# A gated linear scan with top-1 expert routing on one core: second expert product turned round, late zero fills in narrow pieces, expert 0's first product ahead of the branch

## The chip, the cores and the metric

The kernel runs on one core of a Trainium2 chip. Five engines work from queues of their own and wait for each other by semaphores: PE (TensorE, matrix products), DVE (VectorE), ACT (ScalarE), POOL (GpSimd) and SP (SyncE, which here only issues DMAs). The metric is the device time of one execution in microseconds, the median of several runs; smaller is better. One execution was also recorded by the hardware profiler, and all rows below come from it.

## What is computed

The first half is an elementwise recurrence over time, `h = a_t * h + x_gated` per batch row and channel, on arrays of 4 x 5056 x 256 float32. Its result, seen as 20224 tokens of 256 numbers, goes to a layer of 8 experts that keeps at most 80 tokens per expert, those with the largest gate weight; all other rows of the output are zero:

```python
a_t = np.exp(log_a)                       # log_a = 8 * sigmoid(r) * log(sigmoid(a_param))
x_gated = np.sqrt(np.maximum(1.0 - a_t * a_t, 1e-6)) * sig_i * x
for t in range(S):
    h = a_t[:, t] * h + x_gated[:, t]
    y[:, t] = h
...
expert_idx = np.argmax(x @ w_gate, axis=1)          # x: the y of above, one row per token
for e in range(E):
    tok_idx = np.where(expert_idx == e)[0]          # cut to the 80 with the largest gate weight
    h = np.maximum(x[tok_idx] @ w1[e], 0.0)         # 256 -> 1024
    out[tok_idx] = gate_w[tok_idx, None] * (h @ w2[e])   # 1024 -> 256
```

## The kernel before

The time axis is cut into units, 20 of 1024 steps and at the two ends halves and a quarter (u20 has 512 steps, u21, the last, 256). For each unit the kernel loads r, i and x with tokens along the partitions, and does, in this order of dependence: A (PE turns r to channels along the partitions, in two halves, line 123), after tanh T on ACT (line 117); E (ACT takes the exponential into the state array Y, line 126); Q (POOL squares, line 129); S (ACT's square root, line 133); I (ACT's tanh of the i gate, line 137); U (POOL multiplies by x, line 140); B (PE turns the gated input, lines 147 and 148); N (DVE multiplies by the norm, line 151); Y (DVE's scan, line 161). The results stay on the chip in `Y`, 25 slots of [128, 2, 1024]. Steps l and c compute gate weights and expert choices, D stands for PE transposes that keep PE busy and are thrown away (line 231). What comes after what on each engine is the list `ORDER`, written out by hand; a letter with a unit and a half (`E20.0`) is one step.

**Zero fills.** The 20.7 MB of output are first filled with zeros by DMAs from SP's queue, in places that `ORDER` names with Z. A wide fill (line 209) writes 512 tokens, 512 KB, and reads 1024 zeros per partition from `Y[:, 19, 0]`, the slot in which the state of u20 and u21 will stand. A narrow fill (line 215) writes 256 tokens, 256 KB, from the last 256 columns of the same row (`h0`, columns 768 and up), which no unit overwrites. The step `E20.0` sets `st['last']` when its turn in the list comes, so that fills that stand behind it are narrow. `E20.0` and its scan write columns 0 to 511 of that row, and so have to wait until the wide fills have read it. SP's DMAs use eight semaphores in turn, so that a DMA waits for the eighth one before it, and at most eight are under way.

**Choice.** The 16 largest weights of each group are found early and late and combined; the result is `chosen` (token and weight for each slot of each expert).

**Experts.** `front` turns `chosen` into token columns (`col`) and weights (`AT`), with 30 thrown-away transposes on PE behind (`WARM[3]`, line 352). Then the token vectors are gathered: for an expert, ACT copies 32 columns, POOL 24, DVE 24 (`copies`, lines 511 and 512) with addresses that `fetch` (line 505) has loaded into registers. `front` does that for experts 0 and 1. A branch (line 605) then takes the usual case. In `experts`, expert k's `first` is 32 calls of [128 x 64] weights (w1) by 80 tokens, the two 64-column halves of the array side by side (line 550), with `relu` in halves on ACT and DVE (lines 566, 565). `second` is 32 calls in the same shape with w2 as the weights (line 560); its result has channels along the partitions, so ACT copies it to SBUF (`take`, line 567), PE turns it (`turn`, line 571), DVE multiplies by the gate weight (`weigh`, line 573) and POOL scatters 80 rows to the output (line 576). Weights are 2 MB per expert in two buffers; w1 of expert k+2 is asked for when `first(k)` is done, w2 by halves when `second(k)` is. An fp32 product call shows as two MATMULs in the trace (64 for 32 calls), a transpose as one.

Of the kernel before, what the change touches and what calls it, by code (L numbers as in the profile page):

```python
# [64 lines left out]
def moe_kernel(ctx, tc, x, r_gate, i_gate, a_param, w_gate, w1, w2, out, capacity=80):  # L65
# [471 lines left out]
    def experts(own):  # L537

        ps_f = own.enter_context(tc.tile_pool(name="ps_f", bufs=1, space=bass.MemoryType.PSUM))
        hbuf = [rows[:, :FC * CAP], rows[:, FC * CAP:2 * FC * CAP]]  # L540
        turned = [scr[:, (8 + 2 * k) * CAP:(10 + 2 * k) * CAP].rearrange("p (h s) -> p h s", h=2) for k in range(2)]
        res = [scr[:, 1024:1280], scr[:, 1280:1536], scr[:, 1536:1792], scr[:, 1792:2048]]
        phs, pos, outs, sent = {}, {}, {}, []
        def hidden(e): return hbuf[e % 2].rearrange("p (c s) -> p c s", c=FC)
        def first(e, half):
            ph = phs[e, half] = ps_f.tile([P, FC // 2, CAP], F32, name="ph", bufs=3)
            for c in range(half * FC // 2, (half + 1) * FC // 2):
                for h in range(2):
                    for j in range(0, P, P // 2):
                        nc.tensor.matmul(ph[j:j + P // 2, c % (FC // 2)], w1v(e)[:, h, c * P + j:c * P + j + P // 2], XG[:, e % 4, h],  # L550
                                         start=(h == 0), stop=(h == 1), tile_position=(0, j))
            if half and e + 2 < E:
                for g in range(2): load_w1(e + 2, g)
# [26 lines left out]
        for k in range(E):  # L580
            g = k + 2
            if k: take(k - 1)
            if 0 < k < E - 1: copies('A', g - 1, 16, 24)
            first(k, 0); relu(k, 0)
            if 0 < k < E - 1: copies('A', g - 1, 24); copies('V', g - 1, 20)
            first(k, 1); relu(k, 1)
            if k: turn(k - 1); weigh(k - 1)
# [49 lines left out]
```

## Time and profile before

| | us |
|---|---|
| median of 3 runs | 305.67 (305.45 to 306.17) |
| profiled execution | 306.08 |
| its span, first to last instruction | 304.3 |
| PE / DVE / ACT / POOL busy | 252.0 / 210.5 / 230.1 / 202.4 |
| DMA queue of SP | 99.63 MB, 87.1% of 16 engines' span |

All engines are busy about 70 to 80% of the span, so the shares alone name no bound. The kernel has three stretches. From 0 to about 220 us the units run, with the DMA engines busy nearly all the time. From about 220 to 248 us the last choice is made in short dependent steps, with no DMA from 234 us on. From 248 us to the end the eight experts run. A timeline row has the start, the duration (of a group: from its first to its last end), the engine, the line, the operation and its operands, the number, and in brackets the idle time ahead of it and what ended that.

### The profile page before, as it was taken

The page shows a single profiled execution, that of the slowest core. Times are in us where ns is not written, and L with a number is a line of the kernel's source. Part 1 is how long each engine was busy: PE and PEld are TensorE (multiplying, and loading weights), DVE is VectorE, ACT ScalarE, POOL GpSimd, SP SyncE. Part 2 cuts the span into 40 slices and gives each one's busy share as a digit, 9 for nine tenths or more (in the row PEclk, how much of TensorE's full clock was granted, in tenths as well). Part 3 has the DMA queues.
Part 4 walks back from the last instruction along what each step waited for, and adds up shares of the span by engine and source line. Part 5 has one row for each costly group of instructions (what it writes and reads, how often), then busy time and mean ns, then how long its engine had stood idle before and what let it go on. Part 6 is the DMA issues. An engine that isn't in the chain of part 4 may idle for free.

```text
span 304.3 us, 9900 instructions
## 1 busy us (share of the span) xinstructions
PE 252.0 (83%) x3748; PEld 228.0 (75%) x3748; DVE 210.5 (69%) x435; ACT 230.1 (76%) x443; POOL 202.4 (67%) x289
## 2 busy tenths in 40 slices
PE   4968899999899998999799798508979586996882
PEld 3767788898899897988788787407868486986871
DVE  2022069989999999999779889960779566566520
ACT  6999999999989999998998994607703366666510
POOL 2349999899999799899767488032305366777212
PEclk9999999999999999999999999955999787999997
DMA  6999999999999999889999999999997004999941
GB/s 235 407 412 408 409 411 407 408 408 408 407 416 412 365 364 323 325 313 381 409 357 401 310 369 416 408 363 329 308 346 259 1 4 167 300 382 384 360 150 32
DMA packets 38438, 100.99 MB, mean 332 GB/s; under 512 B 3056, under 2 KB 17264, under 8 KB 38384
## 3 DMA queue, kind: packets, MB, share of 16 engines
q1 hardware_dynamic: 38000, 99.63, 87.1%
q8 instruction: 31, 0.51, 0.7%
q0 software_dynamic: 384, 0.66, 0.7%
q14 instruction: 23, 0.19, 0.2%
HBM read 78.91 MB, written 21.36 MB: 330 GB/s over the span
## 4 chain that ended last, share of the span: by engine, by line
ACT 23%; DVE 18%; issue 14%; POOL 13%; DMA 12%; PE 11%; SPq 5%; POOLq 3%; DVEq 0%; ACTq 0%
DVE Y L161 8%; ACT Y L126 8%; POOL Y L512 6%; DVE pu L151 6%; ACT Y L117 5%; SPq L215 4%; ACT Y L133 4%; DMA out_dram<-Y 4%; DMA Y<-in_x_dram 4%; PE pr L123 3%; ACT Y L137 3%; POOLq L505 3%; DMA Y<-in_i_gate_dram 3%; POOL Y L129 2%; PE pu L147 2%
## 5 line engine op out<-in xcount | busy, mean ns | idle before, releaser
L140 POOL TENSOR_TENSOR Y<-Y 128x2048 f32<-128x2048 f32 (+2 forms) x22 | 90.9, 4142 | 20.7 <-DMA Y<-in_x_dram 14.4
L161 DVE TENSOR_TENSOR_SCAN Y<-Y,pu 128x1024 f32<-128x1024 f32 (+8 forms) x50 | 93.3, 1882 | 1.4 <-DMA out_dram<-Y 0.5
L129 POOL TENSOR_TENSOR Y<-Y 128x2048 f32<-128x2048 f32 (+2 forms) x22 | 71.6, 3260 | 28.7 <-ACT Y L126 18.7
L151 DVE SCALAR_TENSOR_TENSOR pu<-Y,pu 128x1024 f32<-128x1024 f32 (+2 forms) x44 | 48.6, 1111 | 52.8 <-PE pu L148 44.7
L148 PE MATMUL pu<-ident,Y 128*128 128x128 f32 x316 | 71.7, 274 | 3.4 <-POOL Y L140 3.4
L147 PE MATMUL pu<-ident,Y 128*128 128x128 f32 x316 | 72.6, 275 | 1.3 <-DVE Y L161 0.5
L123 PE MATMUL pr<-ident,Y 128*128 128x128 f32 x316 | 46.1, 289 | 24.3 <-ACT Y L126 20.0
L123 PEld LDWEIGHTS pr<-ident,Y 128*128 128x128 f32 x316 | 35.8, 146 | 32.6 <-ACT Y L126 27.7
L126 ACT ACTIVATE Y<-pr,tiny 128x1024 f32<-128x1024 f32 (+2 forms) x44 | 49.0, 1113 | 5.6 <-PE pr L123 5.3
L147 PEld LDWEIGHTS pu<-ident,Y 128*128 128x128 f32 x316 | 44.6, 141 | 4.8 <-issue 2.3
L148 PEld LDWEIGHTS pu<-ident,Y 128*128 128x128 f32 x316 | 44.6, 141 | 4.6 <-POOL Y L140 4.6
L231 PE MATMUL pl<-ident 128*128 128x128 f32 x287 | 42.6, 295 | 2.4 <-POOL ident masks.py:199 1.6
L137 ACT ACTIVATE Y<-Y 128x2048 f32<-128x2048 f32 (+2 forms) x22 | 38.2, 1736 | 4.7 <-DMA Y<-in_i_gate_dram 4.6
L511 ACT COPY Y<-Y 128x2 f32 x256 | 26.5, 191 | 18.5 <-issue 10.2
L117 ACT ACTIVATE Y<-Y 128x2048 f32<-128x2048 f32 (+2 forms) x22 | 38.1, 1736 | 2.7 <-DMA Y<-in_r_gate_dram 2.7
L241 PE MATMUL pl<-Y 128*32 128x64 f32 (+2 forms) x1344 | 39.0, 280 | 1.1 <-DVE lg L245 1.1
L231 PEld LDWEIGHTS pl<-ident 128*128 128x128 f32 x287 | 36.5, 154 | 3.2 <-POOL ident masks.py:199 1.6
L133 ACT ACTIVATE Y<-Y 128x2048 f32<-128x2048 f32 (+2 forms) x22 | 37.4, 1734 | 0.7 <-POOL Y L129 0.6
L241 PEld LDWEIGHTS pl<-Y 128*32 128x32 f32 x1344 | 33.9, 124 | 4.6 <-issue 3.2
L512 POOL COPY Y<-Y 128x2 f32 x192 | 24.4, 198 | 11.5 <-issue 6.9
L512 DVE COPY Y<-Y 128x2 f32 x192 | 22.6, 176 | 12.0 <-issue 12.0
L550 PE MATMUL ph<-Y 128*64 128x80 f32 x512 | 20.5, 233 | 4.9 <-issue 4.8
(126 smaller groups left out, 221.9 us busy)
## 6 DMA issues: line engine op xcount, KB each, us to landing
Y<-in_r_gate_dram SPq DMA_DIRECT2D x18, 1024.0 KB, 12.1
Y<-in_x_dram SPq DMA_DIRECT2D x18, 1024.0 KB, 9.3
Y<-in_i_gate_dram SPq DMA_DIRECT2D x18, 1024.0 KB, 9.7
Y<-in_moe_w_dram SPq DMA_DIRECT2D x32, 512.0 KB, 7.2
out_dram<-Y SPq DMA_DIRECT2D x28, 512.0 KB, 9.9
out_dram<-Y SPq DMA_DIRECT2D x23, 256.0 KB, 4.5
Y<-in_r_gate_dram SPq DMA_DIRECT2D x3, 512.0 KB
Y<-in_i_gate_dram SPq DMA_DIRECT2D x3, 512.0 KB
```

The costliest lines, as they stand in the source:

```text
L117: nc.scalar.activation(r, r, AF.Tanh, scale=0.5)
L123: nc.tensor.transpose(pr[:, c0:min(n, g + 512):nb], rr[:, at:at + P], ident)
L126: nc.scalar.activation(state(u, h), prs.pop((u, h))[:, :UNITS[u][2]], AF.Exp, scale=L[:, h:h + 1], bias=L[:, h:h + 1])
L129: nc.gpsimd.tensor_tensor(halves('r', u), a, a, op=ALU.mult)
L140: nc.gpsimd.tensor_tensor(i, i, flat('x', u), op=ALU.mult)
L147: nc.tensor.matmul(cols, xx[:, at:at + P], ident, start=True, stop=False, is_transpose=True)
L148: nc.tensor.matmul(cols, ii[:, at:at + P], ident, start=False, stop=True, is_transpose=True)
L151: nc.vector.scalar_tensor_tensor(pu, halves('r', u)[:, h], 0.5e-3, pu, op0=ALU.max, op1=ALU.mult)
L161: nc.vector.tensor_tensor_scan(y[:, s0:s1], y[:, s0:s1], q[:, s0:s1], init, op0=ALU.mult, op1=ALU.add)
L231: for _ in range(n): nc.tensor.transpose(spare, ident, ident)
L241: nc.tensor.matmul(pl[32 * j:32 * j + 32, s % 2, c0:c0 + n // NR], gates(h, b), Y[:, p, h, o + 4 * j + b:o + n:NR], start=(b == 0 and h == ...
L512: else: eng.tensor_copy(dst, src)
```

## The change

Four things are done.

1. In `ORDER` the fills from `A19.1` on are written z, which is `zero_fill(2)`: two narrow fills in place of one wide. `st['last']` goes. On SP's queue, from the last wide fills that stay to the first expert weights, before:

```order
L209 DMA out_dram<-Y 128x1024 x6
L109 DMA Y<-in_i_gate_dram 128x1024
L109 DMA Y<-in_r_gate_dram 128x1024
L113 DMA Y<-in_r_gate_dram 128x512
L209 DMA out_dram<-Y 128x1024 x4
L109 DMA Y<-in_x_dram 128x1024
L209 DMA out_dram<-Y 128x1024 x5
L113 DMA Y<-in_i_gate_dram 128x512
L113 DMA Y<-in_x_dram 128x512
L215 DMA out_dram<-Y 256x1x256 x22
L304 DMA Y<-in_moe_w_dram 128x1024 x2
```

and after:

```order
L208 DMA out_dram<-Y 128x1024 x6
L109 DMA Y<-in_i_gate_dram 128x1024
L109 DMA Y<-in_r_gate_dram 128x1024
L113 DMA Y<-in_r_gate_dram 128x512
L214 DMA out_dram<-Y 256x1x256 x8
L109 DMA Y<-in_x_dram 128x1024
L214 DMA out_dram<-Y 256x1x256 x10
L113 DMA Y<-in_i_gate_dram 128x512
L113 DMA Y<-in_x_dram 128x512
L214 DMA out_dram<-Y 256x1x256 x22
L303 DMA Y<-in_moe_w_dram 128x1024 x2
```

The nine wide fills around u20's x load became 18 narrow ones in the same places. On ACT, at the table load ahead of `E20.0` (the brackets name the semaphores waited for; DMAHW are the eight of SP's DMAs), before:

```order
L133 ACTIVATE Y<-Y 128x2048 [waits Pool_49]
L126 ACT_TABLE_LOAD [waits DMAHW4_49,DMAHW3_49,DMAHW5_49,DMAHW2_49,DMAHW6_49,DMAHW1_49,DMAHW7_49,DMAHW0_49]
L126 ACTIVATE Y<-pr,tiny 128x512 [waits PE_49] x2
L126 ACTIVATE Y<-pr,tiny 128x256 [waits PE_49]
L133 ACT_TABLE_LOAD
```

and after:

```order
L132 ACTIVATE Y<-Y 128x2048 [waits Pool_49]
L125 ACT_TABLE_LOAD [waits DMAHW5_49,DMAHW6_49,DMAHW4_49,DMAHW7_49,DMAHW0_49]
L125 ACTIVATE Y<-pr,tiny 128x512 [waits PE_49] x2
L125 ACTIVATE Y<-pr,tiny 128x256 [waits PE_49]
L132 ACT_TABLE_LOAD
```

`E20.0` (the 128x512 row) waited there for eight DMA semaphores, and now for five; the narrow fills don't read what it writes.

2. `second` holds relu's result as the weights, [128 x 80], and moves w2, 256 columns: 8 calls per expert in place of 32. Its result has tokens along the partitions; `take` and `turn` go, and `weigh` reads the product from PSUM.

3. `first(0)` stands in `front`, ahead of the branch, and `relu(0)` ahead of the copies for expert 1 (its result goes to a buffer of its own, `hbuf[2]`); the small steps on slots (`rows_of_slots`) move ahead of both. On PE, from the thrown-away transposes to expert 1, before:

```order
L352 MATMUL pd<-ident 128x128 x30
L533 TENSOR_LOAD lg
L605 COMPARE_AND_BRANCH
L550 MATMUL ph<-Y 64x80 x32
L560 MATMUL po<-rows,Y 64x80 x32
L550 MATMUL ph<-Y 64x80 x32
L571 MATMUL pd<-ident,Y 80x128 x2
L560 MATMUL po<-rows,Y 64x80 x32
```

and after (L351 the transposes, L527 first, L562 second):

```order
L351 MATMUL pd<-ident 128x128 x26
L527 MATMUL ph<-Y 64x80 x32
L549 TENSOR_LOAD lg
L598 COMPARE_AND_BRANCH
L562 MATMUL po<-Y 80x256 x8
L527 MATMUL ph<-Y 64x80 x32
L562 MATMUL po<-Y,rows 80x256 x8
```

The branch moved from ahead of expert 0's first product to behind it, and the transposes between the products are gone.

4. `WARM[3]` is 26 in place of 30. In the loop `weigh(k-1)` stands ahead of `first(k)`, and the loads of w1 behind `relu(k, 1)`.

The diff, without what repeats:

```diff
-WARM = (4, 45, 6, 30)
+WARM = (4, 45, 6, 26)
...
-E21.1 I21 N20.0 Z Q21 D5 B20.1 S21.1 c4.1 Y20.0 l19 U21 Z N20.1 c4.2 B21.0 Z Y20.1 c4.3 Z D5 B21.1 N21.0 l20 c4.4 N21.1 Y21.0 Z Y21.1 c4.5
+E21.1 I21 N20.0 z Q21 D5 B20.1 S21.1 c4.1 Y20.0 l19 U21 z N20.1 c4.2 B21.0 z Y20.1 c4.3 z D5 B21.1 N21.0 l20 c4.4 N21.1 Y21.0 z Y21.1 c4.5
...
-        if UNITS[u][0] == PAIRS - 1: st['last'] = True
...
-            if wide and N - a >= 512 and not st.get('last'):
+            if wide and N - a >= 512:
...
+             'l': logits, 'D': idle, 'Z': lambda: zero_fill(1, True), 'z': lambda: zero_fill(2), 'w': gate_weights}
...
+    hbuf = [rows[:, :FC * CAP], rows[:, FC * CAP:2 * FC * CAP], scr[:, 1024:1024 + FC * CAP]]
+    phs = {}
+    def hidden(e): return hbuf[e % 2 if e else 2].rearrange("p (c s) -> p c s", c=FC)
...
-        for k in 'APV': fetch(k, 1); copies(k, 1)
         rows_of_slots()
+        for half in range(2): first(0, half, ps, 2)
+        for k in 'APV': fetch(k, 1)
+        for half in range(2): relu(0, half)
+        for k in 'APV': copies(k, 1)
...
-            if half == 0: pos[e] = ps_f.tile([P, 2, 512], F32, name="po", bufs=2)
+            if half == 0: pos[e] = ps_f.tile([CAP, D], F32, name="po", bufs=2)
             for c in range(half * FC // 2, (half + 1) * FC // 2):
-                for h in range(2):
-                    for j in range(0, P, P // 2):
-                        nc.tensor.matmul(pos[e][j:j + P // 2, h, :CAP], w2v(e)[:, c, h * P + j:h * P + j + P // 2], hidden(e)[:, c],
-                                         start=(c == 0), stop=(c == FC - 1), tile_position=(0, j))
+                nc.tensor.matmul(pos[e], hidden(e)[:, c], w2v(e)[:, c], start=(c == 0), stop=(c == FC - 1))
...
-        def take(e): nc.scalar.copy(turned[e % 2], pos.pop(e)[:, :, :CAP])
-        def turn(e):
-
-            outs[e] = ps_f.tile([CAP, 2 * P], F32, name="pd")
-            for h in range(2): nc.tensor.transpose(outs[e][:, h * P:h * P + P], turned[e % 2][:, h], ident)
         def weigh(e):
-            nc.vector.tensor_scalar_mul(res[e % 4][:CAP], outs.pop(e), AT[:, E + e:E + e + 1])
+            nc.vector.tensor_scalar_mul(res[e % 4][:CAP], pos.pop(e), AT[:, E + e:E + e + 1])
...
+            if k:
+                if k < E - 1: copies('A', g - 1, 16, 24)
+                weigh(k - 1)
+                first(k, 0, ps_f, 3); relu(k, 0)
+                if k < E - 1: copies('A', g - 1, 24); copies('V', g - 1, 20)
+                first(k, 1, ps_f, 3); relu(k, 1)
             if g < E:
+                for h in range(2): load_w1(g, h)
                 for q in 'APV': fetch(q, g)
                 copies('A', g, 0, 16); copies('V', g, 0, 20); copies('P', g)
             if k: scatter(k - 1)
             second(k, 0); second(k, 1)
-        take(E - 1); turn(E - 1); weigh(E - 1); scatter(E - 1)
+        weigh(E - 1); scatter(E - 1)
```

## Rows read from the trace of the kernel before

**Rows 1.** busy time by stretch: us, engines' busy time, granted clock, DMA share, GB/s

```profile
198.00:200.00 2.00, 0.00 (x0) 0.00 (x0) 2.00 (x2) 0.00 (x0) 2.00 (x1) 0.67 1.01 414
...
210.00:212.00 2.00, 2.00 (x11) 2.00 (x11) 0.00 (x0) 1.97 (x3) 0.83 (x1) 0.50 1.05 350
...
234.00:236.00 2.00, 2.00 (x19) 1.81 (x17) 1.97 (x9) 1.43 (x8) 1.46 (x7) 1.00 0.02 8
...
250.00:255.00 5.00, 1.69 (x31) 1.53 (x29) 3.15 (x25) 3.22 (x30) 3.27 (x28) 0.83 0.58 213
...
270.00:275.00 5.00, 4.05 (x99) 3.45 (x94) 3.40 (x24) 3.20 (x31) 3.73 (x25) 1.00 1.06 390
```

**Rows 2.** timeline, ACT: start, duration, line, operation, idle before and releaser

```profile
193.78 1.91 ACT L133 ACTIVATE Y<-Y 128x2048 f32<-128x2048 f32 x1
...
204.75 1.28 ACT L126 ACT_TABLE_LOAD   x1 [9.06 <-DMA out_dram<-Y]
...
211.47 1.06 ACT L133 ACTIVATE Y<-Y 128x1024 f32<-128x1024 f32 x1
...
215.08 0.62 ACT L137 ACTIVATE Y<-Y 128x512 f32<-128x512 f32 x1
```

**Rows 3.** timeline, POOL, same stretch

```profile
197.94 2.34 POOL L140 TENSOR_TENSOR Y<-Y 128x1024 f32<-128x1024 f32 x1 [7.89 <-DMA Y<-in_x_dram]
...
208.94 1.89 POOL L129 TENSOR_TENSOR Y<-Y 128x1024 f32<-128x1024 f32 x1 [8.66 <-issue]
...
216.62 1.30 POOL L140 TENSOR_TENSOR Y<-Y 128x512 f32<-128x512 f32 x1
```

**Rows 4.** timeline, PE, same stretch (MATMULs alone)

```profile
193.00 1.15 PE L231 MATMUL pl<-ident 128*128 128x128 f32 x9
...
209.34 4.14 PE L231 MATMUL pl<-ident 128*128 128x128 f32 x23
```

**Rows 5.** timeline, DVE, same stretch

```profile
214.46 0.69 DVE L151 SCALAR_TENSOR_TENSOR pu<-Y,pu 128x512 f32<-128x512 f32 x1 [11.89 <-PE pu L148]
...
219.53 0.81 DVE L151 SCALAR_TENSOR_TENSOR pu<-Y,pu 128x256 f32<-128x256 f32 x2
```

**Rows 6.** timeline of SP's DMA queue, same stretch

```profile
190.17 4.61 SPq L209 DMA_DIRECT2D out_dram<-Y  x5
...
197.74 21.71 SPq L215 DMA_DIRECT2D out_dram<-Y  x22
```

**Rows 7.** timeline, PE in the expert part

```profile
247.94 2.43 PE L550 MATMUL ph<-Y 128*64 128x80 f32 x64 [0.19 <-issue]
...
253.68 3.88 PE L560 MATMUL po<-rows,Y 128*64 128x80 f32 x64 [3.31 <-ACT rows L566]
...
262.31 2.38 PE L550 MATMUL ph<-Y 128*64 128x80 f32 x64
...
264.62 0.41 PE L571 MATMUL pd<-ident,Y 128*80 128x128 f32 x2
...
264.97 2.43 PE L560 MATMUL po<-rows,Y 128*64 128x80 f32 x64
...
275.26 1.61 PE L550 MATMUL ph<-Y 128*64 128x80 f32 x41 [1.08 <-issue]
```

**Rows 8.** timeline, ACT around the branch and in the first experts

```profile
249.57 3.33 ACT L511 COPY Y<-Y 128x2 f32 x32 [1.83 <-PE ph L550]
...
253.19 0.44 ACT L566 ACTIVATE rows<-ph 128x320 f32<-128x320 f32 x1 [0.29 <-issue]
...
255.38 1.61 ACT L511 COPY Y<-Y 128x2 f32 x16 [1.76 <-issue]
...
258.71 0.44 ACT L566 ACTIVATE rows<-ph 128x320 f32<-128x320 f32 x1
```

**Rows 9.** timeline, the end of the last expert, ACT and POOL

```profile
298.19 0.29 ACT L567 COPY Y<-po 128x160 f32<-128x160 f32 x1 [3.38 <-PE po L560]
...
299.74 0.91 POOL L576 DMA_INDIRECT out_dram<-Y,lg  x1 [2.26 <-DVE Y L573]
```

More of the change, by code (lines that the diff above doesn't have):

```diff
@@ L46 @@
 N17.1 E18.0 U18 c2.7 c3.1 x19@21 c2.8 T19 A18.1 Z Y17.0 Z c3.2 Z E18.1 Z c3.3 I19 Q18 Y17.1 D14 B18.0 Z c3.4 Z c3.5 S18.1 B18.1 U19 c3.6
-A19.0 i20@24 l17 N18.0 E19.0 N18.1 c3.7 Y18.0 D3 A19.1 r20@22 r21@22 E19.1 Z Z Z c3.8 Q19 D8 B19.0 I20 Z Y18.1 T20 T21 t D4 B19.1 S19.1 l18
-x20@21 Z Z Z A20.0 Z Z E20.0 D9 A20.1 U20 i21@24 N19.0 E20.1 x21@21 N19.1 Z D5 A21.0 E21.0 Q20 Y19.0 Z S20.1 Z Y19.1 D23 B20.0 Z A21.1
-E21.1 I21 N20.0 Z Q21 D5 B20.1 S21.1 c4.1 Y20.0 l19 U21 Z N20.1 c4.2 B21.0 Z Y20.1 c4.3 Z D5 B21.1 N21.0 l20 c4.4 N21.1 Y21.0 Z Y21.1 c4.5
-D4 l21 Z c4.6 Z D2 c4.7 c5.1 c4.8 D2 c5.2 c5.3 c5.4 c5.5 c5.6 D25 c5.7 D7 c5.8
+A19.0 i20@24 l17 N18.0 E19.0 N18.1 c3.7 Y18.0 D3 A19.1 r20@22 r21@22 E19.1 z z z c3.8 Q19 D8 B19.0 I20 z Y18.1 T20 T21 t D4 B19.1 S19.1 l18
+x20@21 z z z A20.0 z z E20.0 D9 A20.1 U20 i21@24 N19.0 E20.1 x21@21 N19.1 z D5 A21.0 E21.0 Q20 Y19.0 z S20.1 z Y19.1 D23 B20.0 z A21.1
+E21.1 I21 N20.0 z Q21 D5 B20.1 S21.1 c4.1 Y20.0 l19 U21 z N20.1 c4.2 B21.0 z Y20.1 c4.3 z D5 B21.1 N21.0 l20 c4.4 N21.1 Y21.0 z Y21.1 c4.5
+D4 l21 z c4.6 z D2 c4.7 c5.1 c4.8 D2 c5.2 c5.3 c5.4 c5.5 c5.6 D25 c5.7 D7 c5.8
 """
@@ L519, in rows_of_slots, with first, relu @@
         nc.vector.tensor_tensor(sidx, tk, none, op=ALU.add)
+    hbuf = [rows[:, :FC * CAP], rows[:, FC * CAP:2 * FC * CAP], scr[:, 1024:1024 + FC * CAP]]
+    phs = {}
+    def hidden(e): return hbuf[e % 2 if e else 2].rearrange("p (c s) -> p c s", c=FC)
+    def first(e, half, ps, bufs):
+        ph = phs[e, half] = ps.tile([P, FC // 2, CAP], F32, name="ph", bufs=bufs)
+        for c in range(half * FC // 2, (half + 1) * FC // 2):
+            for h in range(2):
+                for j in range(0, P, P // 2):
+                    nc.tensor.matmul(ph[j:j + P // 2, c % (FC // 2)], w1v(e)[:, h, c * P + j:c * P + j + P // 2], XG[:, e % 4, h],
+                                     start=(h == 0), stop=(h == 1), tile_position=(0, j))
+    def relu(e, half):
+        dst = hidden(e)[:, half * FC // 2:(half + 1) * FC // 2]
+        if half: nc.vector.tensor_scalar_max(dst, phs.pop((e, half)), 0.0)
+        else: nc.scalar.activation(dst, phs.pop((e, half)), AF.Relu)
     def front(ps):
@@ L539, in experts @@
         ps_f = own.enter_context(tc.tile_pool(name="ps_f", bufs=1, space=bass.MemoryType.PSUM))
-        hbuf = [rows[:, :FC * CAP], rows[:, FC * CAP:2 * FC * CAP]]
-        turned = [scr[:, (8 + 2 * k) * CAP:(10 + 2 * k) * CAP].rearrange("p (h s) -> p h s", h=2) for k in range(2)]
         res = [scr[:, 1024:1280], scr[:, 1280:1536], scr[:, 1536:1792], scr[:, 1792:2048]]
-        phs, pos, outs, sent = {}, {}, {}, []
-        def hidden(e): return hbuf[e % 2].rearrange("p (c s) -> p c s", c=FC)
@@ L545, in first, with second @@
-        def first(e, half):
-            ph = phs[e, half] = ps_f.tile([P, FC // 2, CAP], F32, name="ph", bufs=3)
+        pos, sent = {}, []
+        def second(e, half):
+            if half == 0: pos[e] = ps_f.tile([CAP, D], F32, name="po", bufs=2)
             for c in range(half * FC // 2, (half + 1) * FC // 2):
-                for h in range(2):
-                    for j in range(0, P, P // 2):
[L550 to L553, printed above, removed]
@@ L554, in second @@
-        def second(e, half):
-            if half == 0: pos[e] = ps_f.tile([P, 2, 512], F32, name="po", bufs=2)
-            for c in range(half * FC // 2, (half + 1) * FC // 2):
-                for h in range(2):
-                    for j in range(0, P, P // 2):
-                        nc.tensor.matmul(pos[e][j:j + P // 2, h, :CAP], w2v(e)[:, c, h * P + j:h * P + j + P // 2], hidden(e)[:, c],
-                                         start=(c == 0), stop=(c == FC - 1), tile_position=(0, j))
-            if e + 2 < E: load_w2(e + 2, half)
@@ L581, in experts @@
             g = k + 2
[L582 to L587, printed above, removed]
+            if k:
[4 more added lines that the diff above has]
+                first(k, 1, ps_f, 3); relu(k, 1)
             if g < E:
+                for h in range(2): load_w1(g, h)
                 for q in 'APV': fetch(q, g)
```

5 lines of the change are left out of this document (removed).

## Prediction, made before the changed kernel was run

> **What bounds the kernel now.** I read the chain of waits first, for the places where the end of the kernel hangs on a wait; then the timeline of each engine around them, then the busy time by stretch for the DMA rate and PE's granted clock. The change touches two places.
>
> The first is u20. ACT finishes `S19.1` at 193.78 + 1.91 = 195.69 and idles 9.06 us until the last wide zero fill has read the row that `E20.0` overwrites [rows 2]. All else hangs on `E20.0`: POOL's square of u20 idles 8.66 us [rows 3], DVE idles 11.89 us ahead of `N20.0` [rows 5], and PE, out of work from 193.00 + 1.15 = 194.15 on, loses its clock: it falls within 198 to 200 (mean 0.67) and stands at 0.50, the 1.2 GHz level, at 210 to 212, where 23 transposes take 4.14 us in place of the 2.5 us that their pace at full clock gives (9 in 1.15 us, so about 0.11 us each) [rows 1, 4]. DMA runs at 400 GB/s and more, but this stretch waits for it only through that one dependence; from 234 us on it has nothing to do [rows 1].
>
> The second is the expert part, from 247.94 on. Expert 0's relu comes only after ACT's 32 copies for expert 1: the copies run 249.57 to 252.90, the relu at 253.19, and PE idles 3.31 us for it [rows 7, 8]. The mean clock of 250 to 255 is 0.83, and `second(0)` takes 3.88 us where 2.43 is usual [rows 1, 7]. Later the DMA of the weights is the limit: 390 GB/s at a share of 1.06, and `first` broken off for 1.08 us in its middle [rows 1, 7]. The last expert ends with take, turn, weigh and scatter in a row, from 298.19 to the scatter at 299.74 [rows 9].
>
> **The change, part 1: narrow fills.** `E20.0` still names five DMA semaphores, but only wide fills are waited for, and the last of these now stand ahead of u20's i and r loads on SP's queue; those had landed before `S19.1`, since ACT's tanh of r of u20 and u21 stands ahead of it. So I take the wait as gone: 9.06 us. What is late next:
>
> The narrow fills cost queue time. The rate is 414 GB/s with wide and 350 with narrow ones [rows 1]. Four wide fills (2.1 MB) before u20's x load become eight narrow ones: 2.1/0.350 - 2.1/0.414 = +0.9 us, so x lands at 198.8 in place of 197.9 [rows 3]. That load now waits for a nearer one of the eight transfers ahead of it; the queue of seven narrow fills, some 5 us of work, hides it. Ten more narrow fills (2.6 MB) add 1.2 us, so u21's i and x land 2.1 us later: before at about 197.9 + 2.6/0.414 + 0.5/0.4 = 205.5, after at 207.6.
>
> Now the steps. From `E20.0`'s table load at 204.75 to the square at 208.94 were 4.19 us, to the 23 transposes at 209.34 were 4.59 [rows 2 to 4]. From 195.7 these are 199.9 and 200.3, a little less at full clock. But the square stands behind U20 on POOL, 198.8 + 2.34 = 201.1; with 1.89 it ends at 203.0 [rows 3] and the root of 1.06 at 204.1, where it was 212.53 [rows 2]. On PE the pause is now 194.15 to about 198; whether the clock falls in it no row tells, so the transposes end at 202.3 to 204.4 and B20.0 a microsecond later. `N20.0` starts at 204.1 to 205.4 in place of 214.46. From there to `N21.0` at 219.53 were 5.07 us [rows 5], nearly all DVE's own work, which gives 209.2 to 210.5. The other way to `N21.0` is u21's i at 207.6, its tanh 0.62 [rows 2], U21 1.30 [rows 3] and four transposes, 0.4 to 0.5: 210.0. Both say about 210, 9.5 us earlier. I take 9.2, a little less for PE's later half steps; bounds 7 (clock down on, or loads 2 us later) and 10.3.
>
> What follows until 248 us, the choice, is a chain of short steps that no DMA enters, so it moves as a whole. Cover: DMA is done by 234 [rows 1] plus 2.1, 236; expert 0's first product moves from 247.9 [rows 7] to 238.7. The cover is 2.7 us for the last weights and more for the first ones; were it gone, the excess would come off the gain one for one.
>
> **Part 2: the second product turned round.** The trace has no such product. Its price: a transpose of 128 columns takes 0.11 us at full clock, 0.86 ns per column [rows 4]. `first` takes 264.62 - 262.31 = 2.31 us for 64 MATMULs of 80 columns; if the two halves of the array run side by side, that is 32 times 72 ns, 0.90 ns per column [rows 7]. So a MATMUL of 256 columns is 0.22 us, and 8 calls of two each 3.5 us. If the halves do not overlap, a column costs 0.45 ns and the sum is 1.85 us. Two rows agree on the first price, so I take 3.5 us. `turn` and `second` before: 0.35 + 2.3 [rows 7]. PE's work per expert is then 2.3 + 3.5 = 5.8 us, where it was 5.0 and DMA's 2.1 MB at 390 GB/s, 5.4 us, were the limit; experts 2 to 7 took 298.19 - 262.31 = 35.9 us, 6.0 each [rows 7, 9]. The bound goes from DMA to PE, at nearly the same pace.
>
> The Trainium skill speaks against this part: "TensorE: Matmul & The Clock Gate", "Why this matters for your kernels", says that products with few output rows should be laid side by side in column groups of the array. The new form is one product that leaves 48 of 128 columns of the array empty; by that rule PE pays here, and the 0.8 us more per expert above agree.
>
> **Part 3: first(0) ahead, relu before the copies.** Times here are on the axis of before. `first(0)` runs as now from 247.94 to 250.4 [rows 7]; ACT's relu waits only for the fetch, over by 249.57 [rows 8], and is done by 250.0; `second(0)` runs 250.6 to 254.1 at full clock in place of 253.68 to 257.6, a gain of 3.4 us. `first(1)` ends at 256.5. But ACT's own chain has hardly moved: copies for expert 1 now 250.0 to 253.3, branch and fetch 2.5 as from 252.90 to 255.38, then 24 copies for expert 2 at 1.61 per 16 [rows 8], 258.3: only then relu(1), which was at 258.71 [rows 8]. PE idles some 2 us there and `second(1)` ends at 262.3. That is where `first(2)` starts now, 262.31 [rows 7]: the gain is given back. From there six experts at 5.8: `second(7)` ends at 297.1. Before, 1.55 us lay from take to scatter [rows 9]; without 0.29 of take and 0.35 of turn it is 0.9, so the scatter starts at 298.1 in place of 299.74. Gain 1.6; I take 1.3, since each of some 20 waits on PE may cost a little. The 26 warming transposes cost nothing: they end before the columns are there. `weigh` ahead of `first` lies in time in which DVE waits for relu's input.
>
> **Sum.** 9.2 + 1.3 = 10.5. The profiled execution took 306.08 (span 304.30 and 1.78 around it): 295.6. The median is 0.41 below it: 295.2.
>
> **Rivals.**
> (a) The expert part gives back. If PE's 2 us pause before `second(1)` costs the clock, as may be behind the 1.45 us more of `second(0)` [rows 7], or PE's waits add 0.3 us per expert, the 1.3 becomes -1.5: 298.0. For it: ACT (copies 3.3, relu 0.44, fetch 1.75, 5.5 in all [rows 8]), PE at 5.8 and DMA at 5.4 are within 10% of each other.
> (b) Fills too slow. SP's queue gave 22 narrow fills in 21.71 us, 0.99 us each [rows 6]; at that price u21's loads come at 205.5 + 18 x 0.99 - 4.7/0.414 = 212 and `N21.0` at 214.4: gain 5.1 + 1.3, 299.3. Against it: that mean holds a dip around ACT's stall, and the full stretch moves 350 GB/s [rows 1]. A rule points this way: the Trainium skill, "DMA: Bandwidth & Descriptors", "Bandwidth", asks for transfers of 1 MB or more. The 0.99 us for 256 KB of rows 6 agree that small ones are dearer, but not by much.
> (c) The product at 0.45 ns per column: `second` 1.85, ACT's 5.5 us per expert are the limit, and the last two experts, with no copies left, are shorter still: some 4 us more, 291.2.
> (d) Slower. If a moving column costs twice the price above, `second` is 7 us and PE 9.3 per expert, 3.5 us more over six and a half experts: 318. It decides from 7.4 us per expert on, where 1.6 us more times six and a half eat the 10.5. Against it: two rows' price per column.
> (e) The change doesn't do what it says: one of the five transfers that `E20.0` still waits for is late, and the wait stays: 304.
>
> **How the numbers follow.** My forecast (294 to 296.5) 0.62; (a) 0.16; (b) 0.08; (c) 0.09; (d) 0.03; (e) 0.02. A measurement of this kernel can tell about 0.2% (0.6 us) from no change. Faster: all but (d) and part of (e), 0.96; same 0.015; slower 0.025. The range takes in the forecast, (a) and part of (c), 291.8 to 298.4; outside remain (b), (d), (e) and the rest of (c).
>
> **What would show it.** The idle time ahead of the table load before `E20.0` falls from 9.06 to about nothing; `N21.0` at about 210; DMA at rest by 236.5; the first MATMUL of expert 0 at 238 to 239, `second` in 3.4 to 3.7 us; a pause of 1.5 to 2.5 us on PE before `second(1)`, then experts every 5.8 to 6.0 us with PE over 90% busy and the DMA share below 1. It would be wrong if x or i of u20 and u21 are waited for beyond 208, or if PE's clock is down in the expert part.

## The result and the profile after

The changed kernel takes 294.13 us (median of 4 runs, 293.26 to 294.58); the kernel before took 305.92 beside it (4 runs, 305.45 to 307.17). The ratio is 0.9605, 95% interval 0.9568 to 0.9642. A second set, run later (e9 below), gave 294.01 against 305.66, ratio 0.9622 (0.9572 to 0.9672). The forecast was 295.2. Medians are of all runs, ratios of the runs in the chip's usual state; e4, e11 and two of the sets of the kernel before hold one slower run each (the slowest, in e11, 333.74 us).

The profiled execution took 294.16 us, span 292.4, against 306.08 before: 11.92 less. The timeline of the stretch with u20 and u21 (start, duration, queue or engine, line, operation, idle before and what ended it):

```profile
192.41 8.66 SPq L214 DMA_DIRECT2D out_dram<-Y  x10
192.88 1.91 ACT L132 ACTIVATE Y<-Y 128x2048 f32<-128x2048 f32 x1
...
194.81 1.28 ACT L125 ACT_TABLE_LOAD   x1
...
197.50 2.36 POOL L139 TENSOR_TENSOR Y<-Y 128x1024 f32<-128x1024 f32 x1 [6.87 <-DMA Y<-in_x_dram]
...
199.82 1.89 POOL L128 TENSOR_TENSOR Y<-Y 128x1024 f32<-128x1024 f32 x1
...
201.75 1.06 ACT L132 ACTIVATE Y<-Y 128x1024 f32<-128x1024 f32 x1 [0.69 <-POOL Y L128]
...
203.69 0.70 DVE L150 SCALAR_TENSOR_TENSOR pu<-Y,pu 128x512 f32<-128x512 f32 x1 [0.95 <-PE pu L147]
...
205.10 0.63 ACT L136 ACTIVATE Y<-Y 128x512 f32<-128x512 f32 x1 [0.42 <-DMA Y<-in_i_gate_dram]
...
208.31 0.94 DVE L150 SCALAR_TENSOR_TENSOR pu<-Y,pu 128x256 f32<-128x256 f32 x2
```

The table load before `E20.0` follows `S19.1` (192.88 + 1.91 = 194.79) without a pause; the 9.06 us of [rows 2] are gone, and so is POOL's 8.66 before the square [rows 3]. U20 waits for x: POOL idles 6.87 us ahead of it, as it did before (7.89). `N20.0` starts at 203.69 instead of 214.46, `N21.0` at 208.31 instead of 219.53 [rows 5]. `S19.1` itself was 0.90 us earlier than before [rows 2]. Eight of the narrow fills stand ahead of it in `ORDER`, but it starts at 190.91 to 193.78 in the four kernels with wide fills and at 191.60 to 193.48 in those with narrow ones (all runs below), so these 0.90 us are taken as a difference between two executions. Taken off, `N21.0` is 10.3 us earlier.

PE's clock, by stretch (columns as in rows 1: length; busy time and number of instructions of PE, of its weight loads, of DVE, ACT and POOL; granted clock; DMA share; GB/s), and its 23 transposes from the timeline:

```profile
196.00:198.00 2.00, 1.06 (x9) 1.02 (x9) 2.00 (x2) 1.24 (x3) 0.50 (x1) 0.94 1.03 355
198.00:200.00 2.00, 1.90 (x9) 1.54 (x8) 2.00 (x2) 1.20 (x3) 2.00 (x2) 0.50 1.05 356
200.00:202.00 2.00, 2.00 (x15) 2.00 (x14) 2.00 (x2) 1.31 (x2) 1.72 (x1) 0.70 1.04 352
...
234.00:236.00 2.00, 2.00 (x13) 1.86 (x11) 2.00 (x19) 2.00 (x22) 2.00 (x17) 0.67 0.49 168
236.00:238.00 2.00, 0.90 (x24) 0.83 (x25) 1.26 (x10) 1.10 (x12) 0.78 (x6) 1.00 0.06 17
...
270.00:275.00 5.00, 5.00 (x60) 3.64 (x55) 2.77 (x21) 2.71 (x25) 3.56 (x23) 1.00 1.06 378
```

```profile
198.95 3.77 PE L230 MATMUL pl<-ident 128*128 128x128 f32 x23
```

The clock still falls, though PE's pause ahead of `A20.1` is only 2.22 us long (to 196.94): in windows of 0.5 us it is 1.00 up to 197.5, when PE is at work again, then 0.78, and 0.50 from 198 on. The transposes take 3.77 us where [rows 4] had 4.14. DMA moves some 355 GB/s there and comes to rest at about 235. In the experts (270 to 275) PE is busy throughout, where [rows 1] had 4.05 of 5.00 us.

The expert part, timeline:

```profile
230.64 0.23 DVE L537 TENSOR_SCALAR lg<-pv 8x80 int32<-8x80 f32 x1 [0.53 <-PE pv L536]
...
233.60 2.83 DVE L511 COPY Y<-Y 128x2 f32 x24 [2.74 <-issue]
...
237.20 2.44 PE L527 MATMUL ph<-Y 128*64 128x80 f32 x64 [1.10 <-DVE lg L517]
...
238.94 0.44 ACT L532 ACTIVATE Y<-ph 128x320 f32<-128x320 f32 x1 [1.84 <-PE ph L527]
239.27 3.11 ACT L510 COPY Y<-Y 128x2 f32 x32
...
239.61 3.65 PE L562 MATMUL po<-Y 128*80 128x256 f32 x16
...
243.19 2.44 PE L527 MATMUL ph<-Y 128*64 128x80 f32 x64
...
244.76 2.37 ACT L510 COPY Y<-Y 128x2 f32 x24 [2.38 <-issue]
...
247.03 0.43 ACT L532 ACTIVATE rows<-ph 128x320 f32<-128x320 f32 x1
...
247.51 3.68 PE L562 MATMUL po<-Y,rows 128*80 128x256 f32 x16 [1.88 <-ACT rows L532]
...
251.12 2.43 PE L527 MATMUL ph<-Y 128*64 128x80 f32 x64
...
257.10 2.44 PE L527 MATMUL ph<-Y 128*64 128x80 f32 x64
...
287.84 0.91 POOL L568 DMA_INDIRECT out_dram<-Y,lg  x1 [5.06 <-DVE Y L565]
```

`first(0)` starts at 237.20 (before 247.94 [rows 7], 10.74 earlier), `second(0)` follows without the 3.31 us pause, and PE then waits 1.88 us before `second(1)`, because relu(1) stands behind 24 copies on ACT. From `first(2)` on (251.12) an expert takes 5.97 us, 2.36 for `first` and 3.61 for `second`, and PE doesn't pause again. The last scatter is at 287.84 (299.74 in [rows 9]). Between `first(0)` and that scatter lie 50.64 us; before, 51.80.

So the 11.92 us are 0.90 before the stall, 9.84 from `S19.1` to `first(0)`, 1.16 in the expert part, and 0.02 after it.

### The profile page after: what moved, and what is told of

Same layout as the page of the kernel before. It is cut to its first block, busy times and chain, and to the rows that moved or that the text cites. A ratio compares the mean times of both kernels' runs of the same rounds, so it can differ in the third digit from the quotient of the medians.

```text
span 292.4 us, 9077 instructions
## 1 busy us (share of the span) xinstructions
PE 255.0 (87%) x3344; PEld 224.3 (77%) x3344; DVE 209.5 (72%) x435; ACT 228.1 (78%) x435; POOL 202.2 (69%) x289
## 4 chain that ended last, share of the span: by engine, by line
ACT 28%; PE 27%; DVE 20%; issue 11%; DMA 6%; POOL 2%; ACTq 2%; SPq 1%; DVEq 0%; POOLq 0%
DVE Y L160 9%; ACT Y L125 7%; ACT Y L132 6%; DVE pu L150 6%; PE po L562 5%; PE pr L123 4%; ACT Y L136 4%; PE pu L146 4%; DMA Y<-in_i_gate_dram 3%; ACT Y L117 3%; PE pu L147 3%; PE ph L527 3%; PE pl L240 3%; PE pl L230 3%; ACT Y L510 2%
## 5 line engine op out<-in xcount | busy, mean ns | idle before, releaser
L123 PE MATMUL pr<-ident,Y 128*128 128x128 f32 x316 | 45.4, 286 | 15.6 <-ACT Y L125 11.4
L230 PE MATMUL pl<-ident 128*128 128x128 f32 x287 | 41.8, 292 | 2.5 <-POOL ident masks.py:199 1.6
L510 ACT COPY Y<-Y 128x2 f32 x256 | 25.8, 191 | 18.2 <-issue 10.9
L230 PEld LDWEIGHTS pl<-ident 128*128 128x128 f32 x287 | 35.8, 152 | 3.2 <-POOL ident masks.py:199 1.6
L511 DVE COPY Y<-Y 128x2 f32 x192 | 22.0, 177 | 11.7 <-issue 11.6
L562 PE MATMUL po<-Y,rows 128*80 128x256 f32 x112 | 25.8, 383 | 1.9 <-ACT rows L532 1.9
## 6 DMA issues: line engine op xcount, KB each, us to landing
Y<-in_x_dram SPq DMA_DIRECT2D x18, 1024.0 KB, 10.5
```

Of the source, the lines that this page charges most:

```text
L123: nc.tensor.transpose(pr[:, c0:min(n, g + 512):nb], rr[:, at:at + P], ident)
L230: for _ in range(n): nc.tensor.transpose(spare, ident, ident)
```

## The experiments

Twelve more sets of runs were made, one of them (e9) of the changed kernel again. The change has three main parts (narrow fills; turned second product; expert 0's first product ahead of the branch), and with the two kernels themselves all eight combinations were measured, so they come as one table. The stages are from the profiled executions: A is from the start of `S19.1` to `first(0)`, B from `first(0)` to the start of the last scatter; the median of the kernel before, measured beside it, stands in brackets. Of the small steps under 4, `WARM[3]` goes with the third part and the place of `weigh` with the second; the loads of w1 stand in their new place in all but before and e1, which leaves the order of SP's queue as it was.

| fills | second | first(0) | kernel | A | B | time |
|---|---|---|---|---|---|---|
| wide | old | behind | before | 54.16 | 51.80 | 305.92 |
| wide | old | ahead | e12 | 53.62 | 50.02 | 302.42 (305.56) |
| wide | turned | behind | e11 | 52.90 | 54.87 | 306.69 (305.56) |
| wide | turned | ahead | e2 | 52.11 | 52.34 | 304.31 (304.88) |
| narrow | old | behind | e1 | 44.11 | 49.94 | 295.12 (304.88) |
| narrow | old | ahead | e3 | 43.74 | 48.70 | 294.11 (304.88) |
| narrow | turned | behind | e4 | 44.77 | 55.03 | 297.53 (304.88) |
| narrow | turned | ahead | after | 44.32 | 50.64 | 294.13 (305.92) |

**Narrow fills alone (e1), and all but them (e2).** e1 is the kernel before with this, and `z` for `Z` in the table of numbers from u19's last steps on; e2 undoes it in the changed kernel.

```diff
-        if UNITS[u][0] == PAIRS - 1: st['last'] = True
...
-            if wide and N - a >= 512 and not st.get('last'):
+            if wide and N - a >= 512:
```

> The kernel before with the late zero fills narrow and nothing else of the change. By steps (theory): the fills take the wait ahead of E20.0 away and move all that follows up by what the changed kernel showed at expert 0's first product, 10.7 us; the expert part then runs as before, so 295.2 us. Rival: narrow fills end later and push the weights of experts 0 and 1 into the expert part, which is bound by DMA in the old form; then 2 us or more are lost again: 297 us or more.

> The changed kernel with the late fills wide as before, all else as changed. Theory: E20.0 waits 9 us again, the rest of the change is worth the 1.2 us that it gained between expert 0's first product and the last scatter: 304.7 us. Rival: the expert part's gain is larger when the DMA is idle well ahead of it (before, DMA stopped 13 us ahead of the first product, now 2 us): 303 us or less.

e1: 295.12 us, ratio 0.9711 (0.9621 to 0.9801). e2: 304.31, ratio 0.9983 (0.9944 to 1.0021). Both times lie within 0.4 us of the first theories' figures. The steps do so less well: in e1 `first(0)` came 10.35 us earlier and B was 1.86 us shorter, most of it because `second(0)` took 2.43 us instead of 3.88; in e2 B was no shorter than before (why, under Rivals). The timeline of e2 has the old stall:

```profile
204.01 1.28 ACT L126 ACT_TABLE_LOAD   x1 [8.74 <-DMA out_dram<-Y]
```

The fills alone bring 9.8 of the 11.8 us, and without them the gain is gone. Stage A in four kernels with wide fills is 52.11 to 54.16 (mean 53.20), in four with narrow ones 43.74 to 44.77 (44.24): 9.0 us.

**Old second product, the rest as changed (e3).**

```diff
-                nc.tensor.matmul(pos[e], hidden(e)[:, c], w2v(e)[:, c], start=(c == 0), stop=(c == FC - 1))
+                for h in range(2):
+                    for j in range(0, P, P // 2):
+                        nc.tensor.matmul(pos[e][j:j + P // 2, h, :CAP], w2v(e)[:, c, h * P + j:h * P + j + P // 2], hidden(e)[:, c],
+                                         start=(c == 0), stop=(c == FC - 1), tile_position=(0, j))
```

> The changed kernel with the second product, take and turn as before; first(0) and relu(0) stay ahead, fills narrow. Theory: the turned product trades PE time for DMA-bound waits at nearly the same pace, so per expert nothing is won and the tail of the last expert is 0.65 us longer: 294.0 to 295.0 us. Rival: the turned product is what carries the 1.2 us of the expert part: 295.3 us or more.

294.11 us, ratio 0.9664 (0.9586 to 0.9742), in the theory's range. By the times alone it can't be told whether the turned product gains or loses: the interval overlaps that of the changed kernel, and the medians come from different chips. In the profiles (e3's, 291.66 us, is the fastest of its four runs) B is 48.70, 1.94 us shorter than with the turned product. From `first(2)` on the two differ less: 35.93 us with the old, 36.72 with the turned. In e3 PE waits for weights in the later experts, its `first` broken off:

```profile
265.85 0.99 PE L527 MATMUL ph<-Y 128*64 128x80 f32 x23
268.07 1.67 PE L527 MATMUL ph<-Y 128*64 128x80 f32 x41 [1.23 <-issue]
```

**First product behind the branch, the rest as changed (e4).**

```diff
-WARM = (4, 45, 6, 26)
+WARM = (4, 45, 6, 30)
...
-        for half in range(2): first(0, half, ps, 2)
-        for k in 'APV': fetch(k, 1)
-        for half in range(2): relu(0, half)
-        for k in 'APV': copies(k, 1)
+        for k in 'APV': fetch(k, 1); copies(k, 1)
...
+            if k == 0:
+                for half in range(2): first(0, half, ps_f, 3); relu(0, half)
```

> The changed kernel with expert 0's first product and relu behind the branch and the copies for expert 1, with 30 warming transposes, as before; fills narrow and second product turned. Theory: ACT's chain of copies sets when relu(1) comes and gives the 3 us of expert 0 back, so moving it is worth 0.5 us or less: 294.1 to 294.7 us. Rival: it carries the gain of the expert part: 295.3 us or more.

297.53 us, ratio 0.9732 (0.9635 to 0.9829): the rival held. The timeline of PE and the busy time by stretch show a reason that neither theory had:

```profile
238.18 2.44 PE L527 MATMUL ph<-Y 128*64 128x80 f32 x64 [0.38 <-issue]
...
243.96 6.63 PE L559 MATMUL po<-Y 128*80 128x256 f32 x16 [3.34 <-ACT Y L532]
```

```profile
244.00:246.00 2.00, 2.00 (x5) 1.32 (x6) 0.80 (x7) 0.36 (x4) 2.00 (x18) 0.50 0.39 158
246.00:248.00 2.00, 2.00 (x6) 1.15 (x6) 1.55 (x14) 2.00 (x22) 0.94 (x8) 0.50 0.00 0
```

After the 3.34 us pause the granted clock is 0.50, the 1.2 GHz level, and the turned product takes 6.63 us instead of 3.65. The clock costs 3.0 of the 4.4 us by which B grew. The profiled execution took 299.63 us, more than the median; whether the clock fell in the other runs of e4 is not shown.

**Turned product alone (e11); first product ahead alone (e12).** e11 is e4 and e12 is e3, each with wide fills:

```diff
+        if UNITS[u][0] == PAIRS - 1: st['last'] = True
...
-            if wide and N - a >= 512:
+            if wide and N - a >= 512 and not st.get('last'):
```

> The kernel before with the turned second product alone: late fills wide, expert 0's first product and relu behind the branch and behind ACT's copies, as before. Theory 1 (the turned product alone is a loss): PE idles some 3.3 us before second(0) as in the kernel before, the clock falls, and second(0) takes up to 6.6 us (3.88 before, 3.65 at full clock); then experts come every 5.97 us, no faster than before's 6.0. Sum: first(2) 1 to 4 us later, end 0.5 to 3.3 us later: 305.5 to 309. Rival (the prediction's price: 0.8 us more PE per expert, nothing lost at the end, copy and turn saved, DMA the limit in either case): within 0.7 us of the kernel before.

> The kernel before with one part alone: expert 0's first product ahead of the branch and its relu ahead of ACT's copies; late fills wide and second product as before. Theory 1 (this part is a gain of its own with the old product): no pause of 3.3 us before second(0), second(0) in 2.43 us at full clock instead of 3.88, w2's buffer free some 3 us earlier for the weights' DMA, which is the limit from there on; 1 to 2 us faster than the kernel before, 303.7 to 304.7. Rival (ACT gives it back at relu(1), as the prediction had it): within 0.5 us of the kernel before.

e11: 306.69 us, ratio 1.0036 (1.0007 to 1.0066), 0.4% slower than the kernel before and within the first theory's range. Its `second(0)`:

```profile
249.58 6.48 PE L560 MATMUL po<-Y 128*80 128x256 f32 x16 [3.34 <-ACT Y L533]
```

e12: 302.42 us, ratio 0.9883 (0.984 to 0.9925), 3.1 us faster by the medians, which is more than the 1 to 2 us of the first theory. In the profiles 1.78 us are B's, as that theory has it (`second(0)` in 2.44 us, no pause of 3.3 us); of the rest 0.72 lie ahead of `S19.1` and 0.54 in stage A, and no run tells them from spread. The rival (within 0.5 us) did not hold.

**ACT's order (e8, e10), with the changed kernel beside them (e9).** e8 sets ACT's half of each relu ahead of all of ACT's copies for the next expert, and DVE's half, which stood behind all 24 of DVE's copies, behind 8; e10 does the same with the old second product; e9 is the changed kernel unaltered.

```diff
-                if k < E - 1: copies('A', g - 1, 16, 24)
-                weigh(k - 1)
                 first(k, 0, ps_f, 3); relu(k, 0)
-                if k < E - 1: copies('A', g - 1, 24); copies('V', g - 1, 20)
+                if k < E - 1: copies('A', g - 1); copies('V', g - 1, 0, 8)
                 first(k, 1, ps_f, 3); relu(k, 1)
+                weigh(k - 1)
+                if k < E - 1: copies('V', g - 1, 8)
...
-                copies('A', g, 0, 16); copies('V', g, 0, 20); copies('P', g)
+                copies('P', g)
```

> The changed kernel itself, unaltered, so that the kernels of this call have it beside them on the same chip. Theory: the ratio to the kernel before is again 0.957 to 0.964, some 294 us; first(0) at about 237, first(2) about 14 us behind it, then 5.97 us per expert at full clock. It also settles what the turned product is worth: with the second product as before, the profiled run of the same kernel spent 285.60 - 236.90 = 48.7 us from first(0) to the last scatter, the changed kernel 287.84 - 237.20 = 50.6 us; the medians of the two (294.11, 294.13) came from different chips. Theory 1: the turned product is a loss of 1 to 2 us in the expert part, and the changed kernel is slower here than the variants with the old product. Rival: the 1.9 us are a spread of DMA from run to run, and the two are equal within 0.5 us.

> The changed kernel with ACT's relu of each expert ahead of all of its copies for the next one, instead of behind 8 to 24 of them. In the changed kernel PE idles 1.88 us before second(1), because relu(1,0) stands behind 24 copies (2.37 us) on ACT. Theory 1 (the give-back is ACT's order): relu(1,0) goes at the end of its fetch, about 244.8 on that trace's axis, second(1) at about 245.6, the pause is under 0.3 us, and the time falls by 1.7 to 1.9 us against the changed kernel beside it, to about 292.3; the period per expert stays at 5.97. Rival (ACT's work per expert is the limit, whatever its order): the copies, now behind the relu, come late for the next first product; PE idles there instead, and the gain is under 0.5 us.

> The same reordering of ACT with the second product as before (256 rows of w2 stationary, copied and turned). Theory 1 (with the old product PE needs 5.1 us per expert and the weights' DMA, which restarts only when first(0) has freed a buffer and then moves 12.6 MB at 390 GB/s in 32.3 us, is the limit): second(1) comes some 2 us earlier, the weights' DMA therefore too, and the kernel is 0.5 to 2 us below the run with the old product and ACT's old order (294.1): 292 to 293.6; PE still waits for DMA in the last experts. Rival: DMA is at its rate from 240 us on whatever ACT does, and the time stays within 0.4 us of 294.1.

All on one chip, before 305.66: e9 294.01 (0.9622), e8 292.78 (0.9578, 0.9533 to 0.9623), **e10 290.51** (0.9514, 0.947 to 0.9558), the fastest kernel that leaves nothing out, 3.5 us under the changed kernel by the medians. In the profiles 2.7 us of that are B's; what else differs lies outside B, where the edit changes nothing. e9 came as expected, e8 fell less than the first theory said (1.2 us by the medians, not 1.7 to 1.9), and e10 came out below its range. B: e9 50.63, e8 48.69, e10 47.91. In e8 the pause before `second(1)` is gone:

```profile
236.09 2.43 PE L527 MATMUL ph<-Y 128*64 128x80 f32 x64 [0.63 <-ACT Y L510]
...
242.09 2.44 PE L527 MATMUL ph<-Y 128*64 128x80 f32 x64
244.45 3.68 PE L562 MATMUL po<-Y,rows 128*80 128x256 f32 x16
```

The last is 8.36 us behind `first(0)`, where the changed kernel had 10.31, and B falls by the same 1.95 us. The pause had ended with ACT's relu, so ACT's order, not its amount of work, made it. (By the times alone the intervals of e8 and e9 overlap.) In e10 `second(1)` starts 8.35 us behind `first(0)`, the same, but takes 2.43:

```profile
235.94 2.44 PE L527 MATMUL ph<-Y 128*64 128x80 f32 x64 [1.66 <-DVE lg L517]
...
244.29 2.43 PE L565 MATMUL po<-rows,Y 128*64 128x80 f32 x64
```

The rule weighed in part 2 of the prediction (the Trainium skill, "TensorE: Matmul & The Clock Gate", "Why this matters for your kernels": few output rows belong side by side in the array) agrees with e8 against e10: 2.3 us by the medians and 0.8 us by B for the form that it favours, copy and turn included.

**Half of w2's columns (e6).** The second half of the second product is left out, and the output's other columns are a copy.

```diff
-                nc.tensor.matmul(pos[e], hidden(e)[:, c], w2v(e)[:, c], start=(c == 0), stop=(c == FC - 1))
+                nc.tensor.matmul(pos[e][:, :P], hidden(e)[:, c], w2v(e)[:, c, :P], start=(c == 0), stop=(c == FC - 1))
```

> The changed kernel with the second product moving 128 of w2's 256 columns; the other half of its output is a copy of the first half, so half of the second product is left out, and DVE weighs twice. Theory 1 (PE bounds the experts at 0.88 ns per moving column): second takes 1.8 us in place of 3.65, PE needs 4.2 us per expert, and the limit becomes the weights' DMA (12.6 MB at 390 GB/s, 32.3 us) with PE idle in the last experts: last scatter some 2.5 to 4 us earlier, 290 to 291.5. Rival (the period of 5.97 is DMA's or ACT's, and PE merely fills it): second shrinks, the period and the time stay within 0.7 us of the changed kernel's.

289.01 us, ratio 0.9468 (0.9409 to 0.9526); B 45.70, 4.9 us less than in e9 and the changed kernel, more than the first theory's 2.5 to 4. PE ahead of `second(1)` and in its last experts:

```profile
245.70 2.67 PE L562 MATMUL po<-Y,rows 128*80 128x128 f32 x16 [2.23 <-ACT rows L532]
...
270.25 2.30 PE L527 MATMUL ph<-Y 128*64 128x80 f32 x60 [1.07 <-DMA Y<-in_moe_w_dram]
272.48 1.97 PE L562 MATMUL po<-Y,rows 128*80 128x128 f32 x16
...
275.98 2.30 PE L527 MATMUL ph<-Y 128*64 128x80 f32 x60 [1.05 <-DMA Y<-in_moe_w_dram]
```

`second` takes near half (1.97 us; 2.67 in the first row; the granted clock is 0.50 from 247 to 250), so its columns make its price, and from `first(2)` on PE was the bound of the changed kernel. But the starts of `first(2)` to `first(7)` lie 5.18, 4.71, 5.26, 5.38 and 5.73 us apart instead of 5.97: PE waits for ACT's relu in the first of these (0.35 and 0.92 us) and for weights in the later ones, up to 1.07 us. The next bounds are right behind, as the working of the prediction had them.

**The size of a fill (e5).** Single narrow transfers of 512 KB in place of pairs of 256 KB.

```diff
-             'z': lambda: zero_fill(2)
+             'z': lambda: zero_fill(1, False, 2)
...
-            b = min(N, a + ZERO_TOKENS)
+            b = min(N, a + big * ZERO_TOKENS)
```

> The changed kernel with its late zero fills as single transfers of 512 KB (rows of 1 KB from the small zero tile, as the narrow ones) in place of pairs of 256 KB. Theory 1 (what counts is only that these transfers don't read the row that E20.0 writes, not their size): no idle time on ACT before E20.0's table load, the loads of u20 and u21 land within 1 us of where they land in the changed kernel, and the time is that of the changed kernel, 293.4 to 294.6. Rival (the small size itself lets the loads pass: in the kernel before a wide 512 KB fill took 9.9 us from issue to landing, a narrow one 4.5): x of u20 and i of u21 land 1 to 3 us later, U20 and I21 wait for them, 295 to 297.

295.29 us, ratio 0.9679 (0.9626 to 0.9732); A 44.00, B 50.93. No pause before `E20.0` here either, so the stall was the dependence on the row, not the transfer's size. The median lies in the rival's range, but its mechanism isn't shown: U20 started 5.63 us after `S19.1` instead of 4.62, which is inside the 4.49 to 5.82 of the other kernels with pairs of 256 KB, A was not longer, and the interval overlaps those of the changed kernel. Nor does the rate tell: from 196 to 200 us DMA moved 385 GB/s here, with the pairs 356 in the changed kernel and 381 in e9, which is the same kernel.

**Fewer fills (e7).**

Six of the z in `ORDER`, all behind u21's loads, are taken out, and the fill of what is left skips as many tokens:

```diff
+    nz[0] += 12 * ZERO_TOKENS
     zero_fill(-(-N // ZERO_TOKENS))
```

> The changed kernel with 12 of its last zero fills left out (3.1 MB of the output's zeros are not written), none of them ahead of u21's loads. In the changed kernel the engines' registers for expert 0's copies were there 2.9 to 3.3 us after the columns (DVE at 230.64, the copies at 233.60 to 233.97), where it was 2.4 to 2.7 us in the kernel before, whose DMA was idle by then. Theory 1 (the register loads share DMA's or the memory's way with the fills that still run): DMA is at rest at about 226, the copies start 2.4 to 2.7 us after the columns, and first(0) comes some 0.5 us earlier against the choice's steps. Rival (the longer fetch is something else, such as the engines' own queues): the distance stays at 2.9 to 3.3 us.

One run, 293.72 us. DMA was at rest from 226 on, and DVE's copies started 2.36 us after the token columns were written (the register fetch), against 2.96 in the changed kernel; `first(0)` came 5.91 us after the columns instead of 6.56:

```profile
230.38 0.23 DVE L538 TENSOR_SCALAR lg<-pv 8x80 int32<-8x80 f32 x1 [0.52 <-PE pv L537]
232.74 2.81 DVE L512 COPY Y<-Y 128x2 f32 x24 [2.12 <-issue]
```

The first theory fits this, but not all kernels: with DMA running, after, e9, e1 and e10 had 2.84 to 2.96, e6 2.61, and e3, e4, e5 and e8 2.35 to 2.37. So DMA's traffic may be needed for the longer fetch, and is not enough for it. What else enters is open.

## Why the prediction came out right, step by step

The forecast was 1.1 us too high. 0.90 us of the profiled gain lie ahead of the stall, where the prediction had no gain; what the two terms brought is 9.84 + 1.16 = 11.0 us, against 10.5 forecast.

**Narrow fills, 9.2 us: right.** The profiled pair gives 9.84, the four against four profiles 9.0. On the axis of before (0.90 added) `N20.0` came at 204.6 (204.1 to 205.4 forecast) and `N21.0` at 209.2 (about 210). x of u20 came at 198.4 (198.8), i of u21 at 206.0 (207.6): the narrow fills held the loads up less than the working had it. So of the two ways to `N21.0` the loads were not the one that ended last: DVE has no idle time ahead of it, and it follows `N20.0` by 4.62 us of DVE's own work (5.07 before), 0.8 us better than forecast. Some 0.6 of that went again in the register fetch of 2.96 us, where 244.27 - 241.92 = 2.35 were the measure before; the prediction moved the choice "as a whole" and had no such term. DMA's cover held: it was at rest at 235, and no engine waited for expert 0's weights. Whether the clock would fall, left open there, is answered: it fell, just behind the pause.

**Expert part, 1.3 us: the sum right (1.16), in part by luck, and the split not shown by it.** `second` took 3.61 us where 3.5 was worked out (0.88 ns per column), an expert 5.97 where 5.8 was; the pause before `second(1)` was 1.88 (1.5 to 2.5 forecast); DMA's share stayed at 1.06 at 270 to 275, where the prediction looked for less than 1, but PE didn't wait for it. The 5.97 makes some 1.1 us more over six experts than the working had, and the gain expected from there on shrinks by that; what made up for it are 0.45 us kept at `first(2)`, which the working had put at nothing, and the 0.3 held in reserve. The same expert part took 50.63 to 51.20 us in four profiles (after, e9, e5, e7). The term that the prediction never formed is what each part is worth alone. The table gives it by B: the turned product makes it longer in every pair (e12 to e2 2.3, before to e11 3.1, e1 to e4 5.1, e3 to after 1.9), and the first product ahead makes it shorter in every pair (1.2 to 4.4). Since the third part also moves `first(0)`, the border of A and B, the sum A + B is the safer measure, and it has the same signs: 0.8 to 5.8 us longer, 1.6 to 4.8 shorter. Part of both is the clock: it fell ahead of `second(0)` in before, e4 and e11 and in `second(1)` in e2. By the whole time the turned product's loss is clear of the noise in the two pairs with wide fills alone (e11 and before, e2 and e12). The step that hid this is "the bound goes from DMA to PE, at nearly the same pace". From `first(2)` on it holds (36.72 us, and 35.93 to 37.43 with the old product). For experts 0 and 1, whose weights had lain there for long, DMA is no bound, and `second(1)` costs its 3.61 instead of 2.27 us in full; `second(0)`'s excess is hidden by the wait for relu(1), as e3 and after show, whose `second(1)` start alike, 10.50 and 10.31 us behind `first(0)`.

**"The gain is given back": right for the changed kernel, not for the part.** `first(2)` came 13.92 us after `first(0)`, 14.37 before: 0.45 kept of 3.4. With the old product e12 and e3 kept 1.6 (12.77 us). e8 shows who took it: ACT's copies ahead of relu(1).

**Rivals.** (a) exists: e2 had the same pause, and behind it the clock fell (0.56 at 257 to 258, 0.50 at 258 to 260):

```profile
255.80 5.37 PE L563 MATMUL po<-Y,rows 128*80 128x256 f32 x16 [1.89 <-ACT rows L533]
```

It cost 1.7 us, in one of five profiles with such a pause (after, e9, e2, e5, e7: 1.85 to 1.90 us), and made the 1.2 us of the expert part a loss of 0.5. What decided it is not shown, so that both profiles of the changed kernel kept the clock may be luck. (b) didn't come: `N21.0` came at 209.2, not 214.4. (c) and (d) are excluded by 0.88 ns per column. (e) is excluded by the timeline.

## What to carry to other kernels

A transfer that reads a buffer which the program overwrites later is a hidden order; taking it from a buffer that nobody writes removed 9 us without a faster instruction anywhere. When a change has several parts, price each by itself at the place where its resource is the bound: here one part paid for another's loss, and the kernel without that part, with ACT's relu ahead of its copies, is 3.5 us faster, 2.7 of it in the expert part. Order the short step that a busy engine's next product waits for ahead of the long ones on its own queue.

## What the runs showed that was not expected

The same pause does not always cost PE its clock. Of 3.31 to 3.34 us, ahead of `second(0)`, it was lost in before, e4 and e11, and kept in e1, whose granted clock is 1.00 throughout from 239 to 252:

```profile
243.34 2.43 PE L559 MATMUL po<-rows,Y 128*64 128x80 f32 x64 [3.32 <-ACT rows L565]
```

(This profile is the fastest of e1's four runs; the others have no trace.) Of 1.85 to 1.90 us ahead of `second(1)` it was kept four times and lost once, and of 2.23 us (e6) lost. Behind such a pause a product of 3.65 us took 6.63, 6.48 and 5.37 us (e4, e11, e2), one of 2.43 us took 3.88 (before). What decides between keeping and losing no run here isolates.

The register fetch for the copies took 2.35 to 2.37 us in all kernels whose DMA was idle then (before, e2, e7, e11, e12); with DMA at work it took that in four (e3, e4, e5, e8), 2.61 in e6, and 2.84 to 2.96 in four others (after, e9, e1, e10).
